# A sliding-window attention with a feed-forward layer: fewer idle matmuls, another order of loads, zeroing on GpSimd

## The chip, the cores and the metric

The kernel runs on one core of a Trainium2 chip. The metric is the device time of one execution in microseconds. Five runs of the kernel before were timed, and one execution was taken by the hardware profiler; all times on engines below come from that one.

## The reference

Attention over 8 batches of 8 heads, 576 positions and 64 numbers a head, with a causal mask: the first four heads see the last 32 positions, the other four see every fourth of the last 128. Then a feed-forward layer with a squared ReLU on the 4608 x 512 result.

```python
rel = pos[:, None] - pos[None, :]
mask_plain = (rel >= 0) & (rel < 32)
mask_dil = (rel >= 0) & (rel < 32 * 4) & (rel % 4 == 0)
scores = np.where(mask, scale * q @ k.T, -1e9)
attn = softmax(scores)
x = (attn @ v)            # heads side by side: 4608 x 512
h = np.maximum(x @ w_in, 0.0)      # w_in: 512 x 2048
out = (h * h) @ w_out              # w_out: 2048 x 512
```

## The kernel before

All order is written by hand. `PROGRAM` (lines 21 to 36) is a text of short codes, cut by `|`. What stands ahead of the first `|` is issued first; the part behind the (g+1)-th `|` is issued after feed-forward group g. An engine runs what it was given in that order, and waits where it needs another engine or a load. I write g0, g1 and so on for the groups.

**The groups.** The feed-forward layer works on tiles of tokens, 256 for the first four tiles and 512 after them. A group of the first product (`mm1`, L667) takes two columns of blocks of w_in at 256 tokens; its result is put through ReLU on ScalarE (L678) and squared on VectorE (L679). A group of the second product (`g2`, L699) is four 128x512 matmuls with one quarter of w_out: `part` p reads quarter p. After the fourth quarter ScalarE copies the sum (L705, to `osb`) and SyncE stores it. Groups g0 to g15 are the first product of tiles 0 and 1; g16 to g23 are the second product of tile 0, in the order quarter 0, 1, 0, 1, 2, 3, 2, 3 (two halves of the tile taken in turn). So g20 is the first to read w_out's third quarter and g21 the first to read its last. g24 to g31 are the second product of tile 1. Groups g2 and g3 are the first to read w_in's second quarter.

**The loads.** q, k, v and the weights come through GpSimd's DMA queue, which changes float32 to bfloat16 on the way. Codes such as `L1:q00123` mean: of batch 1, q and k of part 0, heads pairs 0 to 3 (two DMAs, L161). Part 0 is the first 256 positions of a batch, part 1 the other 320. `L0:i0` to `i3` are quarters of w_in (L753), `L0:o0` to `o3` quarters of w_out (L758), `v..d`, `p` and `r` are pieces of v (L184 or L191, L178, L197). q and k go to staging tiles `qb` and `kb`, of which there are three pairs (`rb`); batch 1 has the second, batches 0 and 2 share the first. v goes to `vd` and to the block-diagonal tile `vbd`, of which batches take two in turn.

**Batch 0, ahead of the groups (`first_step`).** For a pair of heads e and a part: `T` transposes q and k on TensorE (L495), `C` copies the result out of PSUM (`C..a` on ScalarE and VectorE, `C..v` on VectorE alone; L502 to L510), `B` writes the mask as a large negative number into a PSUM tile, with a matmul of the identity (L536), `S` adds the scores onto it (L555), `E` takes the exponential on ScalarE (L560), `P` and `D` are the products with v and with ones (L586, L602), `L`, `X` and `M` make the reciprocal and the product (L609, L612 on ScalarE, L619 on VectorE) and write `xT`, which group g0 reads. `B` takes one of four PSUM buffers named `pf` and needs nothing but the mask; the buffer comes free when an earlier `E` has read it.

**Idle matmuls.** `w21` and `W2`, `W3` and so on call `turn` (L457): that many matmuls of a zero tile, whose result nobody reads, 256 columns wide for `w` and 128 for `W`.

```python
elif code[0] in "wW":
    turn(int(code[1:]), 256 if code[0] == "w" else P)
```

**Batch 1 and later (`step`).** `1q2` is: q of head pair 2 of batch 1, part 0: transposes on TensorE (L235) into one of two PSUM buffers `pa`, then four copies (L248) on ScalarE for pairs 0 and 1, on VectorE for 2 and 3. `1k2` is the same for k (L252 or L259, VectorE). Capital letters are part 1. `1v3` spreads v on VectorE (L207), `1a2` is scores, exponential and mask (L310 or L304, L314, L315), `1o2` the product with v and its scaling (L413 to L428); `b` and `p` are `a` and `o` of part 1.

**Zeroing.** `z` zeroes the halves of the second `vbd` outside the diagonal blocks (`zero_halves`, L716 and L717). `y` zeroes rows 64 to 79 of part 0 in the staging tiles of batches 1 and 2 (L771, L772), since the transposes of a step read 80 rows. Both are VectorE work, issued after g15 and g17.

Of the kernel before, what the change touches and what calls it, by code (L numbers as in the profile page):

```python
# [19 lines left out]

PROGRAM = (
    "L0:q001 L0:q023 L0:q101 L0:q123 L0:v0d L0:v0p L0:i0 L0:v1dr L0:i1 L0:v1p L0:i2 L0:i3 L0:o0 L0:o1 L0:o2 "
    "L1:q00123 L0:o3 w21 T00 C00a T10 C10a B00 B10 W2 S00 E00 W3 S10 E10 W5 T20q W10 T20k C20v T30 C30v B20 "
    "B30 W3 S20 E20 W3 S30 E30 T01 C01v T11 C11v B01 B11 W2 S01 E01 T21 C21v S11 E11 T31 C31v B21 B31 P20 P30 "
    "D20 D30 L20 X20 M20 P00 P10 D00 D10 L00 X00 M00 S21 E21 S31 E31 W8 | | P21 P31 D21 D31 L21 X21 M21 L31 "
    "X31 M31 | | P01 P11 D01 D11 L01 X01 M01 L11 X11 M11 | | | | | | | | | | | | z | | y L1:v0dp L1:q10123 "
    "L1:v1dpr | | | | L2:q00123 L2:q10123 1q1 1q3 | 1q2 | 1k2 | 1k1 1v3 | 1a2 | 1v2 1k0 1q0 | 1o2 | 1a0 1a1 | "
    "1k3 1o0 1o1 | 1a3 1Q0 | 1K0 1o3 | 1Q1 1K1 | 1Q2 | 1b0 | | 1Q3 1K2 L2:vwpdr L3:q00123 L3:q10123 | L2:x | | "
    "2q0 | | 2k0 1V2 | 1b2 1p0 | 1b1 1V3 1K3 | | 1p2 1p1 | 2a0 1b3 | 2k1 2o0 2b0 1p3 | 2q1 2k2 L3:x | | 2q2 "
    "2p0 L3:vwpdr 2a1 | | | 2b1 | 2o1 2q3 2a2 | | 2p1 2v2 | 2k3 | 2b2 2o2 | 2v3 | 2a3 2p2 L4:q10123 | 2b3 3k1 "  # L30
    "| 2o3 3q1 | | 3a1 L4:q00123 2p3 | 3k0 3k2 | | 3o1 | | | 3q0 3v2 | | | | 3a0 | 3b1 3k3 | | | 3p1 L4:x 3q2 "
    "L4:vwpdr | | 3b0 | 3a2 3q3 3o0 4k0 | | | 3o2 3b2 | | 3p0 3v3 | 4q1 3a3 | 3p2 4q2 4q0 | L5:q10123 3b3 | "
    "3o3 | 4k1 | | L5:q00123 3p3 4k2 4k3 4a0 L5:vwpdr | | | 4b0 | | 4q3 | | 4o0 | | | 4a2 4v2 | 4b2 | 4a3 L5:x "
    "4a1 | 4o2 | | | 4p2 L6:q00123 4v3 | | 4b1 | | 4p0 | | 4p1 | 5q0 5k0 | 4b3 | | | | 4o1 | | 5k2 L6:q10123 "
    "4o3 | 5q2 5k1 | | 4p3 | 5q1 |"
)


# [25 lines left out]
def kernel(  # L64
# [9 lines left out]
    nc = tc.nc  # L74
    P = nc.NUM_PARTITIONS
    B, H, S, D = q.shape
# [66 lines left out]
    vbd = [const.tile([P, NE, NB, P], bf16, name=f"vbd{i}") for i in range(2)]  # L143
# [6 lines left out]
    def staged(b: int, nm: str):  # L150


        t = rb[STAGE[b]][nm]
        return t[:, :].rearrange("p (a h x) -> p a h x", h=H, a=2)

    def load_qk(b: int, part, es):
        hs = slice(2 * es[0], 2 * es[-1] + 2)
        for nm, src in (("q", q), ("k", k)):
            t = staged(b, nm)
            t0, n = RES * MS[part], MN[part]  # L160
            nc.gpsimd.dma_start(  # L161
                t[0:n, part, hs, :], src[b, hs, t0 : t0 + RES * n, :].rearrange("h (p r) d -> p h (r d)", r=RES)
            )

    def load_v(b: int, parts, which="pdr"):


        dst = vbd[b % 2]
        if b not in vds:
            vds[b] = vd_pool.tile([P, NE // 2, 2, RES * D], bf16, name="vd")  # L170
        p0, p1 = parts[0], parts[-1] + 1
        i0, i1 = 4 * p0, 4 if p1 == 1 else NB
        sides = [(hl, slice(64 * hl, 64 * hl + 64)) for hl in range(2)]
        for what in which:
            if what == "p":
                for e in range(NE // 2):
                    for hl, rows in sides:
                        nc.gpsimd.dma_start(  # L178
                            dst[rows, e, i0:i1, rows],
                            v[b, 2 * e + hl, 64 * i0 : 64 * i1, :].rearrange("(i p) d -> p i d", p=64),  # L180
                        )
            elif what == "d" and len(parts) == 1:
                for hl, rows in sides:
                    nc.gpsimd.dma_start(  # L184
                        vds[b][rows, :, p0, :],
                        v[b, H // 2 + hl : H : 2, 256 * p0 : 256 * p1, :].rearrange("e (p r) d -> p e (r d)", r=RES),
                    )
            elif what in "d01":
                for e in (0, 1) if what == "d" else (int(what),):
                    for hl, rows in sides:  # L190
                        nc.gpsimd.dma_start(  # L191
                            vds[b][rows, e, :, :],
                            v[b, H // 2 + 2 * e + hl, 0:512, :].rearrange("(m p r) d -> p m (r d)", p=64, r=RES),
                        )
            elif p1 == 2:
                for hl, rows in sides:
                    nc.gpsimd.dma_start(  # L197
                        dst[rows, NE // 2 : NE, 8, rows],
                        v[b, H // 2 + hl : H : 2, 512:S, :].rearrange("h p d -> p h d"),
                    )  # L200
# [231 lines left out]
    def step(b: int, code: str):  # L432

        what, e = code[0], int(code[1])
        part = int(what in "QKVbp")
        if what in "qk" and (b > XB or b == XB and e >= NE // 2):
            t = (qx if what == "q" else kx)[b % 2]
            by_act = what == "q" and e < NE // 2 and b < ADDED  # L440
            halves(
                e, what, t[:, 2 * e : 2 * e + 2, :, :], 0, M, nc.scalar.copy if by_act else nc.vector.tensor_copy
            )
        elif what in "qQkK":
            trans(b, e, what.lower(), part)
        elif what in "vV":
            spread_v(b, e, [part] if b in PARTED else [0, 1])
        elif what in "ab":
            scores(b, e, part)
        elif b in PARTED and e % 2:  # L450
            pv(b, e, part, ps_f, "pf")
        else:
            pv(b, e, part)
# [4 lines left out]
    def turn(n: int, cols: int):  # L458


        if "W" not in first:
            pool, nm = (ps_f, "pf") if ("P", 2, 0) in first else (ps_o, "po")
            first["W"] = pool.tile([P, 512], f32, name=nm)
        for _ in range(n):
            nc.tensor.matmul(
                first["W"][:, 0:cols], idle[:, 0:P], idle[:, 0:cols], start=True, stop=True, skip_group_check=True
            )
# [247 lines left out]
    def zero_halves(t):  # L715
        nc.vector.memset(t[0:64, :, :, 64:128], 0.0)  # L716
        nc.vector.memset(t[64:128, :, :, 0:64], 0.0)  # L717
# [45 lines left out]
    def cross_all(b):  # L763
        for part in range(2):
            for nm in "kq":
                cross(b, nm, part)

    def run(code):
        if code == "y":
            for nm in "qk":  # L770
                nc.vector.memset(staged(1, nm)[64:80, 0, :, :], 0.0)  # L771
                nc.vector.memset(staged(2, nm)[64:80, 0, 0 : H // 2, :], 0.0)  # L772
        elif code == "z":
            zero_halves(vbd[1])
        elif code[0] in "wW":
            turn(int(code[1:]), 256 if code[0] == "w" else P)
        elif code[0] in "TCBSEPDXM" or code[0] == "L" and code[2:3] != ":":
            first_step(code)
        elif code[0] != "L":
            step(int(code[0]), code[1:])  # L780
        else:
            b, what, part, which = int(code[1]), code[3], code[4:5], code[5:]
            if what == "q":
                load_qk(b, None if part == "w" else int(part), [int(e) for e in which])
            elif what == "x":
                cross_all(b)
            elif what == "v":
                load_v(b, [0, 1] if part == "w" else [int(part)], which)
            else:
                (load_w_in if what == "i" else load_w_out)(int(part))  # L790
# [22 lines left out]
    for code in program[0]:  # L813
        run(code)
    for g, group in enumerate(groups):
        for b in [x for x in CROSS if CROSS[x] == g]:
            cross_all(b)
        for b in [x for x in LOAD_V if LOAD_V[x] == g]:
            load_v(b, [0, 1])
        for b in [x for x in LOAD_QK if LOAD_QK[x] == g]:  # L820
            for part in range(2):
                load_qk(b, part, [0, 1, 2, 3])
        group()
        for code in program[g + 1] if g + 1 < len(program) else ():
            run(code)
        while steps and steps[0][0] <= g:
            step(*steps.pop(0)[1:])
# [30 lines left out]
```

## Time and profile before

| What | Value |
|---|---|
| five runs | 314.54, 318.08, 315.33, 317.29, 315.55 us; median 315.55 |
| the profiled execution | 314.54 us, its span 312.7 us |
| idle matmuls, 256 columns (L465) | 21, 4.3 us from 1.06 us on |
| idle matmuls, 128 columns (L465) | 28 into `po`, 2.7 us, and 8 into `pf`, 0.6 us |
| VectorE memsets z and y | 6, from 36.94 to 42.48 us |
| DMA issues on GpSimd, o3 | 24.55 us, lands 16.4 us later |
| DMA issues on GpSimd, q and k of batch 1, part 0 | 23.17 and 23.87 us, land 14.3 and 15.1 us later |

The page gives busy shares of each engine. PE is TensorE's matmuls and PEld its weight loads, which run beside them; DVE is VectorE, ACT ScalarE, POOL GpSimd, SP SyncE. A row of the timeline merges neighbouring instructions of a kind: its start, its length, engine, line, operation, output and input, count, and in brackets the idle time of the engine before it and what ended that. "x8" are eight instructions. The ends of matmuls are modelled, so rows of TensorE overlap a little. The time to landing is counted from the start of a DMA's issue.

### The profile page before, as it was taken

The page shows a single profiled execution, that of the slowest core. Times are in us where ns is not written, and L with a number is a line of the kernel's source. Part 1 is how long each engine was busy: PE and PEld are TensorE (multiplying, and loading weights), DVE is VectorE, ACT ScalarE, POOL GpSimd, SP SyncE. Part 2 cuts the span into 40 slices and gives each one's busy share as a digit, 9 for nine tenths or more (in the row PEclk, how much of TensorE's full clock was granted, in tenths as well). Part 3 has the DMA queues.
Part 4 walks back from the last instruction along what each step waited for, and adds up shares of the span by engine and source line. Part 5 has one row for each costly group of instructions (what it writes and reads, how often), then busy time and mean ns, then how long its engine had stood idle before and what let it go on. Part 6 is the DMA issues. An engine that isn't in the chain of part 4 may idle for free.

```text
span 312.7 us, 6856 instructions
## 1 busy us (share of the span) xinstructions
PE 302.9 (97%) x2605; PEld 190.0 (61%) x2605; DVE 200.3 (64%) x641; ACT 193.8 (62%) x416; POOL 87.0 (28%) x136
## 2 busy tenths in 40 slices
PE   8989989999999999999999999999999999999994
PEld 5779746968755555555499655555555555445543
DVE  6435587898987888985799469946995334104400
ACT  6377427859978956785478547864686456216511
POOL 8774276564265037401451041000000000000000
PEclk9999999999999999999999999999999999999999
DMA  8999999999979989995699975602200210121022
GB/s 115 155 166 214 204 145 179 184 135 200 152 141 193 180 106 214 141 187 66 89 140 140 141 120 100 109 4 66 69 0 2 68 68 2 34 67 36 0 67 67
DMA packets 79808, 34.91 MB, mean 112 GB/s; under 512 B 49824, under 2 KB 74784, under 8 KB 79776
## 3 DMA queue, kind: packets, MB, share of 16 engines
q0 software_dynamic: 47680, 18.36, 52.2%
q1 hardware_dynamic: 31952, 15.93, 26.1%
q8 instruction: 20, 0.33, 0.4%
q10 hardware_dynamic: 144, 0.20, 0.2%
q14 instruction: 12, 0.10, 0.1%
HBM read 36.90 MB, written 9.44 MB: 148 GB/s over the span
## 4 chain that ended last, share of the span: by engine, by line
PE 78%; DMA 10%; ACT 5%; POOL 3%; issue 2%; DVE 1%; ACTq 0%; POOLq 0%
PE pf L699 36%; PE pf L667 33%; DMA w_out_sb<-in_moe_w_out_dram 5%; PE po L413 3%; PE pd L415 2%; DMA w_in<-in_moe_w_in_dram 2%; DMA vd<-in_v_dram 2%; PE pa L304 2%; PE pa L310 1%; ACT qT L248 1%; POOL qb L161 1%; ACT h2T L678 1%; POOL kb L161 1%; PE pa L235 1%; ACT rec L417 1%
## 5 line engine op out<-in xcount | busy, mean ns | idle before, releaser
L699 PE MATMUL pf<-w_out_sb,h2T 128*128 128x512 bf16 (+1 forms) x592 | 134.8, 373 | 1.5 <-DMA w_out_sb<-in_moe_w_out_dram 1.0
L667 PE MATMUL pf<-xT,w_in 128*128 128x256 bf16 (+1 forms) x768 | 133.9, 326 | 1.8 <-DVE xT L619 1.2
L667 PEld LDWEIGHTS <-w_in 128*128 128x128 bf16 x768 | 82.4, 113 | 37.5 <-issue 2.8
L678 ACT ACTIVATE h2T<-pf 128x512 bf16<-128x512 f32 x144 | 83.7, 597 | 24.7 <-PE pf L667 23.7
L699 PEld LDWEIGHTS <-h2T 128*128 128x128 bf16 x592 | 54.2, 98 | 54.8 <-issue 1.9
L679 DVE TENSOR_TENSOR h2T<-h2T 128x512 bf16<-128x512 bf16 x144 | 57.9, 423 | 40.5 <-ACT h2T L678 39.0
L705 ACT COPY osb<-pf 128x512 f32<-128x512 f32 (+1 forms) x37 | 21.2, 573 | 47.3 <-PE pf L699 47.2
L428 DVE TENSOR_TENSOR xT<-po,rec 128x288 bf16<-128x288 f32 (+2 forms) x52 | 23.7, 456 | 31.5 <-ACT rec L418 30.9
L178 POOL DMA_DIRECT2D vbd<-in_v_dram x40 | 28.2, 725 | 52.3 <-PE pd L415 44.3
L417 ACT ACTIVATE rec<-pd 128x288 f32<-128x288 f32 (+2 forms) x52 | 21.5, 413 | 23.9 <-PE pd L415 22.9
L314 ACT ACTIVATE pt<-pa 128x352 bf16<-128x352 f32 (+6 forms) x56 | 27.6, 499 | 7.8 <-PE pa L310 4.1
L418 ACT ACTIVATE rec<-rec 128x288 f32<-128x288 f32 (+2 forms) x56 | 24.8, 443 | 1.8
L413 PEld LDWEIGHTS <-vbd 128*128 128x128 bf16 x286 | 17.0, 97 | 9.9 <-issue 0.7
L248 DVE COPY qT<-xx 64x288 bf16<-64x288 bf16 x80 | 19.9, 249 | 1.1
L161 POOL DMA_DIRECT2D qb<-in_q_dram x18 | 12.9, 719 | 23.0 <-DMA xx<-qb 17.6
L252 DVE COPY kbd<-xx 64x288 bf16<-64x288 bf16 x40 | 18.8, 470 | 0.6
L413 PE MATMUL po<-pt,vbd 128*128 128x96 bf16 (+3 forms) x263 | 18.0, 198 | 0.3 <-DVE vbd L207 0.2
L191 POOL DMA_DIRECT2D vd<-in_v_dram x24 | 14.5, 626 | 10.2 <-DMA qb<-in_q_dram 5.5
L415 PE MATMUL pd<-pt,mk 128*128 128x96 bf16 (+5 forms) x158 | 16.3, 204 | 0.0
L161 POOL DMA_DIRECT2D kb<-in_k_dram x18 | 12.8, 709 | 1.8 <-DMA w_out_sb<-in_moe_w_out_dram 1.2
L197 POOL DMA_DIRECT2D vbd<-in_v_dram x16 | 9.6, 604 | 11.0 <-PE pd L415 7.5
L304 PE MATMUL pa<-qT,kbd 128*128 128x96 bf16 (+2 forms) x146 | 12.2, 201 | 0.5 <-ACT qT L248 0.5
(81 smaller groups left out, 229.7 us busy)
## 6 DMA issues: line engine op xcount, KB each, us to landing
out_dram<-osb SPq DMA_DIRECT2D x18, 128.0 KB, 3.4
qb<-in_q_dram POOLq DMA_DIRECT2D x7, 320.0 KB, 7.5
kb<-in_k_dram POOLq DMA_DIRECT2D x7, 320.0 KB, 8.4
vd<-in_v_dram POOLq DMA_DIRECT2D x32, 64.0 KB, 6.0
w_in<-in_moe_w_in_dram POOLq DMA_DIRECT2D x4, 512.0 KB, 6.9
w_out_sb<-in_moe_w_out_dram POOLq DMA_DIRECT2D x4, 512.0 KB, 12.8
qb<-in_q_dram POOLq DMA_DIRECT2D x7, 256.0 KB, 5.6
kb<-in_k_dram POOLq DMA_DIRECT2D x7, 256.0 KB, 8.3
```

The costliest lines, as they stand in the source:

```text
L161: nc.gpsimd.dma_start(t[0:n, part, hs, :], src[b, hs, t0 : t0 + RES * n, :].rearrange("h (p r) d -> p h (r d)", r=RES))
L178: nc.gpsimd.dma_start(dst[rows, e, i0:i1, rows], v[b, 2 * e + hl, 64 * i0 : 64 * i1, :].rearrange("(i p) d -> p i d", p=64),)
L248: copy(qT[rows, e, :, m0 : m0 + n].rearrange("p (c j) m -> p j c m", j=2)[:, jj, :, :], src)
L314: nc.scalar.activation(pt[:, off : off + n], ps[:, 0:n], ACT.Exp, scale=SCALE)
L413: nc.tensor.matmul(oo, vb[:, e, i, :], rh, start=(x == 0), stop=(x == len(mms) - 1), skip_group_check=True)
L417: nc.scalar.activation(rec[:, 0:n], d[:, 0:n], ACT.Ln)
L418: nc.scalar.activation(rec[:, 0:n], rec[:, 0:n], ACT.Exp, scale=-1.0)
L428: nc.vector.tensor_tensor(out=tok, in0=o if o is o3 else o[:, 0:n], in1=rec if o is o3 else rec[:, 0:n], op=ALU.mult)
L667: nc.tensor.matmul(acc[u][:, nt * x + y0 : nt * x + y1], w_in_sb[piece][:, kt, c0 : c0 + 509 : 4], xT[:, kt, t0 : t0 + y1 - y0], start=(kt ...
L678: nc.scalar.activation(hv, acc[u][:, :].rearrange("p (x n) -> p x n", x=per), ACT.Relu)
L679: nc.vector.tensor_tensor(out=hv, in0=hv, in1=hv, op=ALU.mult)
L699: nc.tensor.matmul(cur[m][:, c0:c1], h2[:, f, P * m : P * m + P], w_out_sb[:, f, c0:c1], start=(f == 0), stop=(f == NF - 1),)
```

## The change

The text of codes is changed in its first stretch and around g15 to g23, and the zeroing moves to GpSimd.

- `L0:o3` stands ahead of `L1:q00123` (two DMAs) instead of behind it.
- `z`, `y` and then `L1:v0dp`, `L1:q10123` and `L1:v1dpr` are issued right after `L1:q00123`, ahead of batch 0's work, instead of after g15 and g17. On GpSimd's own queue the order of the loads stays the same but for o3; the six memsets are new there, between `L1:q00123` and `L1:v0dp`.
- `B20`, `B30`, `B01`, `B11` and `B21` come earlier among batch 0's steps, `B31` comes later, behind `M00`. The 128-column idle matmuls go from 36 to 16: W2, W3, W5, W10, W3, W3, W2, W8 become W5, W2, W3, W2, W4. `w21` stays.
- `1q1 1q3` are issued after g22 instead of g21, `1q2` after g23 instead of g22, in one place with `1k2`. From `1k1 1v3` on (after g24) all is as before.

```diff
-"... L0:o0 L0:o1 L0:o2 L1:q00123 L0:o3 w21 T00 C00a T10 C10a B00 B10 W2 S00 E00 W3 S10 E10 W5 T20q W10
- T20k C20v T30 C30v B20 B30 W3 S20 E20 W3 S30 E30 T01 C01v T11 C11v B01 B11 W2 S01 E01 T21 C21v S11 E11
- T31 C31v B21 B31 P20 P30 D20 D30 L20 X20 M20 P00 P10 D00 D10 L00 X00 M00 S21 E21 S31 E31 W8 | ...
- z | | y L1:v0dp L1:q10123 L1:v1dpr | | | | L2:q00123 L2:q10123 1q1 1q3 | 1q2 | 1k2 | 1k1 1v3 | ..."
+"... L0:o0 L0:o1 L0:o2 L0:o3 L1:q00123 z y L1:v0dp L1:q10123 L1:v1dpr w21 T00 C00a T10 C10a B00 B10 S00 E00
+ B20 S10 E10 B30 T20q B01 W5 T20k C20v T30 C30v B11 W2 S20 E20 W3 S30 E30 T01 C01v T11 C11v W2 S01 E01 T21
+ C21v B21 S11 E11 T31 C31v P20 P30 D20 D30 L20 X20 M20 P00 P10 D00 D10 L00 X00 M00 B31 S21 E21 S31 E31 W4
+ | ... | L2:q00123 L2:q10123 | 1q1 1q3 | 1q2 1k2 | 1k1 1v3 | ..."
@@ run(code)
         if code == "y":
             for nm in "qk":
-                nc.vector.memset(staged(1, nm)[64:80, 0, :, :], 0.0)
-                nc.vector.memset(staged(2, nm)[64:80, 0, 0 : H // 2, :], 0.0)
+                nc.gpsimd.memset(staged(1, nm)[64:80, 0, :, :], 0.0)
+                nc.gpsimd.memset(staged(2, nm)[64:80, 0, 0 : H // 2, :], 0.0)
         elif code == "z":
-            zero_halves(vbd[1])
+            nc.gpsimd.memset(vbd[1][0:64, :, :, 64:128], 0.0)
+            nc.gpsimd.memset(vbd[1][64:128, :, :, 0:64], 0.0)
```

## The prediction, on record before the result was known

> **What bounds the kernel now.** I read the page's busy shares first, then the table of stretches, then what TensorE waits for, and last the timeline around the two places that the change touches.
>
> ```profile
> PE 302.9 (97%) x2605; PEld 190.0 (61%) x2605; DVE 200.3 (64%) x641; ACT 193.8 (62%) x416; POOL 87.0 (28%) x136
> ```
> ```profile
> 10.00:15.00 5.00, 4.62 (x136) 3.56 (x135) 2.80 (x9) 1.91 (x4) 3.92 (x7) 1.00 1.28 145
> 17.50:20.00 2.50, 1.58 (x14) 1.42 (x14) 0.79 (x2) 1.85 (x4) 1.81 (x4) 1.00 1.33 187
> 30.00:35.00 5.00, 5.00 (x48) 5.00 (x47) 2.54 (x6) 3.34 (x7) 1.23 (x2) 1.00 1.10 208
> 40.00:45.00 5.00, 3.57 (x30) 1.85 (x30) 4.02 (x13) 1.71 (x6) 3.82 (x7) 1.00 1.34 134
> 100.00:160.00 60.00, 59.97 (x459) 34.04 (x458) 49.35 (x165) 41.02 (x88) 21.67 (x34) 1.00 1.01 140
> ```
> The columns are the stretch, its length, the busy time of PE, PEld, DVE, ACT and POOL, the granted clock, the DMA share and GB/s. TensorE is the bound almost everywhere: of 312.7 us it leaves 9.8 open, nearly all before 100 us and at the very end. So a microsecond taken from TensorE's path before 100 us reaches the end only if nothing else there is just as tight. The clock is 1.00 in every stretch, also where TensorE stood for 0.92 us of 2.50.
>
> TensorE's waits after 17 us (line, releaser, us, times, longest):
> ```profile
> PE pf L667 <- DVE xT L619: 1.2, 3, 0.8
> PE pf L699 <- DMA w_out_sb<-in_moe_w_out_dram: 1.0, 1, 1.0
> PE pa L235 <- ACT qT L248: 0.5, 1, 0.5
> ```
> The timeline in the head, and around the second and third of those waits (start, us, engine, line, what; in brackets the idle time before it and what ended it):
> ```profile
> 8.44 0.73 PE L465 MATMUL po<-idle 128*128 128x128 bf16 x10
> 9.10 0.31 PE L495 MATMUL pa<-mk,kb 64*64 64x64 bf16 x8
> ...
> 14.81 0.44 PE L586 MATMUL po<-pt,vd 64*64 64x64 bf16 x16
> ...
> 21.89 1.94 PE L667 MATMUL pf<-xT,w_in 128*128 128x256 bf16 x16
> ...
> 36.94 1.02 DVE L716 MEMSET vbd<- 64x1152 uint32 x1 [0.18 <-issue]
> 39.42 0.91 DVE L771 MEMSET qb<- 16x1024 uint32 x1 [0.16 <-issue]
> 40.94 1.02 PE L699 MATMUL pf<-w_out_sb,h2T 128*128 128x512 bf16 x4 [0.96 <-DMA w_out_sb<-in_moe_w_out_dram]
> 42.00 0.59 ACT L705 COPY osb<-pf 128x512 f32<-128x512 f32 x1 [5.70 <-PE pf L699]
> 42.49 1.07 ACT L248 COPY qT<-pa 64x128 bf16<-64x128 bf16 x4
> 42.50 0.93 DVE L248 COPY qT<-pa 64x128 bf16<-64x128 bf16 x4
> 43.61 0.30 PE L235 MATMUL pa<-mk,qb 80*128 80x80 bf16 x4 [0.49 <-ACT qT L248]
> 43.95 0.92 DVE L248 COPY qT<-pa 64x128 bf16<-64x128 bf16 x4 [0.53 <-PE pa L235]
> 49.70 0.50 PEld L304 LDWEIGHTS <-kbd 128*128 128x128 bf16 x8 [0.18 <-DVE kbd L252]
> ```
> And two pieces of the chain that ended last (start, us, what):
> ```profile
> 14.80 7.04 DMA w_in<-in_moe_w_in_dram
> ...
> 24.55 16.36 DMA w_out_sb<-in_moe_w_out_dram
> ```
> TensorE stands 0.96 us at 39.98 for the last quarter of w_out (group g21). And w_in's second quarter (i1), issued at 14.80, lands at 21.84, 0.05 us before g2, the first group that reads it, starts at 21.89.
>
> **The change part by part.** The sum is made against the profiled execution: 314.54 us, of which the span is 312.7; the median of the five runs shown is 1.01 us above it.
>
> *Idle matmuls and masks.* Ahead of P20 the idle 128-column matmuls fall from 28 to 12 (2+3+5+10+3+3+2 against 5+2+3+2), and from W8 to W4 behind E31. Ten of them move what follows from 8.44 to 9.10, so one is 66 ns: 16 x 66 = 1.06 us. Every B step is still run, but B31 (half of the 0.54 us from 14.27 to 14.81) moves behind M00, 0.27 us. Against this S01 has nothing left to hide its wait for the VectorE copies C01 (B01 and B11 stood there), some 0.5 us, and the first W2 only becomes part of the wait for the copies at 6.98. The transfers allow the advance: q and k of the first heads' second part landed at 8.5 and 10.0 (T01 ran at 10.84), those of T21 at 10.9 and 11.7 (12.53), v for P20 at 13.4 (14.81). So P20 goes from 14.81 to some 13.4 to 14.2, and with it the two ScalarE and VectorE chains that end at 18.80. But g2 needs i1, which the change does not touch: all loads up to o2 stay as they were on GpSimd's queue. TensorE then waits 0.6 to 1.3 us at 21.84 where it waited for nothing. I cost this part at 0.05 us gained. The cover is i1's landing; were it gone, the gain would be 1.3, and without any advance it is 0. Behind g2 all is tied to g2 (P01, D01, the 0.30 us wait at 26.88), so nothing comes back there.
>
> A rule speaks against this part. The rows give clock 1.00 in all stretches. The Trainium skill, "TensorE: Matmul & The Clock Gate", part 1, says that a window of about 3.4 us without activity halves TensorE's clock, and a busy one of that length restores it. My longest new gap is 1.3 us, so the row and the gap give 0; were one window nevertheless judged idle, an estimate from that page is half of 3.4 us, 1.7 us lost, and then only if it fell behind g2. I take 0 and keep 1.7 for the range.
>
> *w_out's last quarter (o3) ahead of batch 1's first q and k.* The queue lands in order: o2 at 36.4 (22.7 + 13.7), q at 37.5 (23.17 + 14.3), k at 39.0 (23.87 + 15.1), o3 at 40.9. Each of the 512 KB quarters o1 and o2 took 2.5 to 3.1 us after the one before it, o3 behind q and k 1.9. So o3 now lands at 38.3 to 39.5, ahead of 39.98, and the 0.96 us go. q and k land at 39.5 to 41.0 instead. What is late next: 1q1 and 1q3, now behind g22 (39.98 + 2 x 0.86 = 41.70), need q; 1k2 at about 43.4 needs k. Both have 1.5 us and more.
>
> What follows is the step that decides. 1q1 at 41.70 is only 0.1 us earlier than before (41.80). Its ScalarE copies started at 42.49 because the osb copy at 42.00 stood before them; that copy now belongs to g21's end at 40.85 and is over. So they run from about 42.05 to 43.12, and 1q2, which needs that PSUM buffer, comes at 43.16 instead of 43.61. From there VectorE is the bound: the copies of 1q2, 1k2, 1k1, 1v3, the mask of 1a2, 1v2 and 1k0 filled it from 43.95 to 49.65 with hardly a gap, and 1a0 waited for the last of them at 49.70. Begun at 43.5, the same 5.70 us end at 49.2. Of the 1.45 us of TensorE waits (0.96 + 0.49) only 0.45 to 0.5 thus reach 50 us; the rest turns into short waits for VectorE and ScalarE between 43 and 49. After 50 us the chain runs through compute alone, so the 0.5 is carried. Batch 2's transposed q and k are landed by 71 and first read at 76.4, those of batch 3 by 88.5 against some 92.6.
>
> *Zeroing (z, y).* VectorE loses 2 x 1.02 + 2 x 0.91 + 2 x 0.48 = 4.82 us between 36.94 and 42.48. It had nothing else there; only its first copy (42.50) came some 0.2 us late, contained in the above. GpSimd gets six memsets behind q and k of batch 1 (last issue over at 25.16) and ahead of L1:v0d. Its row has no such memset (only 128x1 ones, 0.10 us). From below: the VectorE rows, 4.8 us, or less. From above: the Trainium skill, "GPSIMD Engine Reference", section "Elementwise — side-by-side cycle accounting", puts its best tight loop at 1.8 cycles an element, and the engine at 1.2 GHz; for 2 x (2304 + 2048 + 1024) = 10752 bf16 elements a partition that is an estimate of 16.1 us, and at the 2.6 cycles that it gives for two inputs 23.3. The nearest row is VectorE's, so I take 5 to 10. Queued behind them are two loads v0d, four v0p, q and k of part 1, then batch 2's. They were issued at 26.02, 28.61, 31.05, 34.18, 36.68, 37.72, 39.27 and 41.19, each held back for an older transfer, and GpSimd stood idle for 10.4 of the 14.1 us from 25.2 to 39.3 (0.86 + 1.97 + 1.85 + 2.51 + 1.89 + 0.43 + 0.93). With 9 us of memsets the first goes at 34.4 and the queue has caught up by 37; they land behind k at 41 anyway, as before. Cost 0, hidden by the backlog o0 to k. The memsets need not wait for q's and k's landing: the v0p loads were issued from 31.05 on, before the memset at 36.94 that stands before them in the program and touches other rows and columns of the same tile, so disjoint regions make no wait.
>
> Sum: -0.05 - 0.45 + 0 = -0.5 us. Span 312.2, that execution 314.0, median 315.05.
>
> **The rivals.** *All of both waits comes through:* if the copies are less tight than I read them, 0.96 + 0.49 and 0.05 are gained, 314.05; if i1 also came early, up to 1.3 more, 312.8. For it: the chain names TensorE at most of 43.6 to 51; against it: the wait for VectorE at 49.70. *Nothing changes:* q or VectorE late by another half microsecond takes the 0.5 back, 315.5. *Slower:* the memsets hold GpSimd's queue. v0d's second load goes at 25.2 + T + 1.2 and lands 4.8 us later (as q at 39.27 did once the backlog was gone); 1v3 wants it at 46.6, and VectorE is in order, so 1k0 stands behind it. From T = 15.4 us each microsecond of T costs about one. At 16.1 it is 0.7, at 20 4.6 (319.6), at 23.3 7.9. It passes 1% above 315.55 from T = 19. Against it: 19 us is four times the VectorE rows.
>
> **How the numbers follow.** -0.5: 0.55. All comes through: 0.2, of which 0.05 beyond 1%, with the runs' scatter. Nothing: 0.1. Held queue or a clock window: 0.15, of which 0.12 over 1%. One percent is 3.2 us, what the five runs (314.54 to 318.08) can just tell from no change. So faster 0.05, same 0.83, slower 0.12. I predict 315.0; the range is 313.0 to 317.6: below, the full gain and some scatter, above, the lost 1.7 or T near 17.
>
> **What would show it.** Right: no wait of L699 for w_out at 40; a new wait of L667 for w_in of 0.6 to 1.3 us ending near 21.8; 1q2 near 43.2 and short waits for VectorE up to 49; GpSimd memsets of 5 to 10 us in all from 25.2, and v0p loads back at their times by 37. Wrong: g2 well before 21.8, memsets over 15 us, VectorE waiting for vd at 46, a clock below 1.00, or w_out still waited for.

## The result: 0.6% faster, nearly four times the gain that was forecast

The changed kernel took 313.75 us (median of 38 executions, 313.16 to 319.84), the kernel before 315.93 us (75 executions beside it, 313.99 to 319.04). The ratio is 0.9941, 95% interval 0.9926 to 0.9955, or 1.4 to 2.3 us gained. The forecast was 0.5 us, within 1%; 313.75 lies in the range of 313.0 to 317.6.

The profiled execution of the changed kernel took 313.40 us, its span is 311.4 us. The page's busy shares, as before:

```profile
PE 302.8 (97%) x2585; PEld 188.4 (61%) x2585; DVE 195.8 (63%) x635; ACT 194.1 (62%) x416; POOL 96.3 (31%) x142
```

What TensorE waited for between 17 and 100 us (line, releaser, us, times, longest):

```profile
PE pf L667 <- DVE xT L619: 1.0, 2, 0.7
...
PE pf L667 <- DMA w_in<-in_moe_w_in_dram: 0.2, 1, 0.2
...
PE pa L235 <- ACT qT L248: 0.2, 1, 0.2
```

The row for w_out is gone, and the 0.49 us in front of 1q2 are 0.16. The timeline at the places shown of before, with g16 to g21 in one row without a stop:

```profile
14.13 0.44 PE L586 MATMUL po<-pt,vd 64*64 64x64 bf16 x16
...
17.03 0.41 PE L667 MATMUL pf<-xT,w_in 128*128 128x256 bf16 x2 [0.24 <-DMA w_in<-in_moe_w_in_dram]
...
18.12 1.69 PE L667 MATMUL pf<-xT,w_in 128*128 128x256 bf16 x14 [0.68 <-DVE xT L619]
...
21.13 1.92 PE L667 MATMUL pf<-xT,w_in 128*128 128x256 bf16 x16
...
34.73 6.21 PE L699 MATMUL pf<-w_out_sb,h2T 128*128 128x512 bf16 x28
...
41.12 1.08 ACT L248 COPY qT<-pa 64x128 bf16<-64x128 bf16 x4 [0.42 <-PE pa L235]
...
42.25 0.30 PE L235 MATMUL pa<-mk,qb 80*128 80x80 bf16 x4 [0.16 <-ACT qT L248]
...
43.57 0.32 PE L235 MATMUL pa<-mk,kb 80*128 80x80 bf16 x4
...
48.56 0.49 PE L304 MATMUL pa<-qT,kbd 128*128 128x96 bf16 x8
```

and of before, g16 to g20 and 1a0:

```profile
35.50 4.48 PE L699 MATMUL pf<-w_out_sb,h2T 128*128 128x512 bf16 x20
...
49.86 0.48 PE L304 MATMUL pa<-qT,kbd 128*128 128x96 bf16 x8
```

P20 starts at 14.13 (before: 14.81), g2 at 21.13 (21.89), g16 at 34.73 (35.50), 1q2 at 42.25 (43.61), 1a0 at 48.56 (49.86). Of the 1.3 us at 1a0 about 0.8 were there at g2 and 0.5 came at w_out. From there the difference stays 1.3 us to the end of the spans (312.7 and 311.4). So between these two executions both halves of the change act, the head (all up to g15) and the place of o3, while the forecast gave the head 0.05 us. GpSimd's rows from the timeline:

```profile
24.22 2.08 POOL L774 MEMSET vbd<- 64x2304 bf16 x1
26.34 2.01 POOL L775 MEMSET vbd<- 64x2304 bf16 x1
28.30 1.80 POOL L771 MEMSET qb<- 16x2048 bf16 x1
30.05 0.94 POOL L772 MEMSET qb<- 16x1024 bf16 x1
30.94 1.80 POOL L771 MEMSET kb<- 16x2048 bf16 x1
32.69 0.94 POOL L772 MEMSET kb<- 16x1024 bf16 x1
33.58 1.22 POOL L184 DMA_DIRECT2D vd<-in_v_dram  x2
...
36.54 0.61 POOL L178 DMA_DIRECT2D vbd<-in_v_dram  x1 [0.49 <-DMA w_out_sb<-in_moe_w_out_dram]
```

The six memsets take 9.57 us, and the loads behind them are back at their old times by 36.54 (third v0p, before 36.68). The next ones, the fourth v0p and q and k of part 1, go at 39.00, 40.42 and 41.71, later than before (37.72, 39.27, 41.19). That is not the memsets: in the changed kernel with the zeroing on VectorE they go at 38.84, 40.31 and 41.64.

### The profile page after: what moved, and what is told of

It reads as the page before. It is cut to its first block, busy times and chain, and to the rows that moved or that the text cites. A ratio compares the mean times of both kernels' runs of the same rounds, so it can differ in the third digit from the quotient of the medians.

```text
span 311.4 us, 6816 instructions
## 1 busy us (share of the span) xinstructions
PE 302.8 (97%) x2585; PEld 188.4 (61%) x2585; DVE 195.8 (63%) x635; ACT 194.1 (62%) x416; POOL 96.3 (31%) x142
## 4 chain that ended last, share of the span: by engine, by line
PE 87%; ACT 6%; DVE 4%; issue 2%; ACTq 0%
PE pf L667 37%; PE pf L699 37%; PE po L413 3%; PE pd L415 2%; PE pa L304 2%; PE po L465 2%; PE pa L310 1%; ACT h2T L678 1%; ACT qT L248 1%; DVE kbd L252 1%; PE pa L495 1%; ACT rec L417 1%; PE pa L235 1%; ACT rec L418 1%; DVE xT L428 1%
## 5 line engine op out<-in xcount | busy, mean ns | idle before, releaser
L428 DVE TENSOR_TENSOR xT<-po,rec 128x288 bf16<-128x288 f32 (+2 forms) x52 | 23.7, 457 | 31.0 <-ACT rec L418 30.5
```

The costliest lines, as they stand in the source:

```text
L428: nc.vector.tensor_tensor(out=tok, in0=o if o is o3 else o[:, 0:n], in1=rec if o is o3 else rec[:, 0:n], op=ALU.mult)
```

## The experiments

Ten kernels ran beside the changed one, and two of the kernels twice, each with the kernel before on the same chip. "Full clock" are the executions whose mean granted clock was at least 0.9975; the last column counts the others, most of them at 0.993 to 0.995, a few at 0.988 to 0.992.

| Kernel | median us | ratio to before (95%) | median at full clock | below full clock |
|---|---|---|---|---|
| before, in the three sets | 316.4, 316.3, 316.5 | 1 | 315.7, 315.7, 315.8 | 53 of 151 |
| changed | 313.75 | 0.9941 (0.9926 to 0.9955) | 313.6 | 9 of 39 |
| changed, again | 313.54 | 0.9918 (0.9892 to 0.9944) | 313.5 | 2 of 15 |
| masks alone | 316.19 | 1.0010 (0.9991 to 1.0028) | 315.6 | 11 of 22 |
| o3 alone | 314.14 | 0.9946 (0.9927 to 0.9966) | 314.1 | 0 of 7 |
| zeroing alone | 316.89 | 1.0013 (0.9992 to 1.0033) | 315.9 | 13 of 22 |
| changed, without the masks | 314.42 | 0.9953 (0.9932 to 0.9973) | 314.4 | 2 of 22 |
| changed, g2 without i1 | 313.68 | 0.9917 (0.9895 to 0.9939) | 313.6 | 4 of 22 |
| the same, without the masks | 314.06 | 0.9935 (0.9908 to 0.9963) | 314.1 | 0 of 10 |
| changed, 1q1 behind g21 | 313.66 | 0.9929 (0.9908 to 0.9951) | 313.5 | 3 of 22 |
| changed, zeroing on VectorE | 313.44 | 0.9914 (0.9882 to 0.9946) | 313.4 | 0 of 6 |
| the same, again | 313.33 | 0.9906 (0.9875 to 0.9938) | 313.3 | 0 of 6 |
| before, o3 later | 318.51 | 1.0067 (1.0044 to 1.0091) | 317.0 | 16 of 20 |
| before, wait filled | 316.46 | 0.9992 (0.9970 to 1.0013) | 316.5 | 0 of 14 |

### The masks alone

```diff
- w21 T00 C00a T10 C10a B00 B10 W2 S00 E00 W3 S10 ... S31 E31 W8
+ w21 T00 C00a T10 C10a B00 B10 S00 E00 B20 S10 ... S31 E31 W4
```

> Only the steps of batch 0 are reordered and the idle matmuls go from 36 to 16; o3 stays behind q and k, zeroing stays on VectorE. My theory after the result: the masks bring g2 forward by 0.6 to 0.8 us (from 21.9 to about 21.2), but alone they gain nothing, since o3 still lands near 40.9: TensorE then stands about 1.7 us for w_out at g21 instead of 0.96, ratio 0.998 to 1.001. My prediction's step (g2 is held by i1's landing near 21.84): g2 at 21.8, wait for w_out 1.0, ratio 1.000. Rival, that the whole gain comes from the head: ratio near 0.994.

Nothing is gained (1.001), as the theory after the result said, but not quite for its reason. The two largest waits of TensorE in this profile from 15 to 100 us:

```profile
PE pf L699 <- DMA w_out_sb<-in_moe_w_out_dram: 1.9, 1, 1.9
PE pf L667 <- DMA w_in<-in_moe_w_in_dram: 1.6, 2, 1.0
```

and the timeline:

```profile
17.50 2.04 PE L667 MATMUL pf<-xT,w_in 128*128 128x256 bf16 x16 [0.97 <-DMA w_in<-in_moe_w_in_dram]
...
21.82 1.94 PE L667 MATMUL pf<-xT,w_in 128*128 128x256 bf16 x16 [0.64 <-DMA w_in<-in_moe_w_in_dram]
...
41.81 1.02 PE L699 MATMUL pf<-w_out_sb,h2T 128*128 128x512 bf16 x4 [1.90 <-DMA w_out_sb<-in_moe_w_out_dram]
```

In this execution the head's gain went, as the prediction said, into waits for w_in, 0.97 for the first quarter and 0.64 for the second; and whatever had passed would have ended in the wait for o3.

### o3 alone

```diff
- L1:q00123 L0:o3
+ L0:o3 L1:q00123
```

> Only o3 stands ahead of q and k of batch 1; 1q1 and 1q3 stay behind g21. My theory: no wait for w_out at g21 (0.96 gone), VectorE then carries about 0.5 us of it past 50 us, ratio about 0.9984 (-0.5 us). Rival, that all of the two waits comes through: -1.4 us, 0.9955. Rival, that q is late for 1q1 at 40.85: no gain, with a wait of L235 for qb.

0.9946, 1.7 us: about the rival's number, and most of the whole change. But not for the rival's reason. In its timeline g16 to g21 now run without a stop, and 1q2 still waits:

```profile
36.17 5.34 PE L699 MATMUL pf<-w_out_sb,h2T 128*128 128x512 bf16 x23
...
43.16 0.30 PE L235 MATMUL pa<-mk,qb 80*128 80x80 bf16 x4 [0.49 <-ACT qT L248]
...
49.97 0.49 PE L304 MATMUL pa<-qT,kbd 128*128 128x96 bf16 x8
```

From g16 to 1a0 it is 13.80 us here, 13.83 in the changed kernel (34.73 to 48.56) and 14.36 before (35.50 to 49.86): of the 0.96 some 0.55 get past the copies, as I said, and q was there in time for 1q1. What was larger than I said must be the wait itself.

### How large is the wait for o3?

In five profiles of kernels with o3 behind q and k, device time less the start of g21 is nearly the same: before 314.54 - 40.94 = 273.6, masks alone 315.84 - 41.81 = 274.0, zeroing alone 317.19 - 42.81 = 274.4, wait filled 316.68 - 42.80 = 273.9, o3 later 316.96 - 43.38 = 273.6. In all five g21 waits for o3; two of the rows, of zeroing alone and of wait filled:

```profile
42.81 1.02 PE L699 MATMUL pf<-w_out_sb,h2T 128*128 128x512 bf16 x4 [1.68 <-DMA w_out_sb<-in_moe_w_out_dram]
```

```profile
42.80 1.02 PE L699 MATMUL pf<-w_out_sb,h2T 128*128 128x512 bf16 x4 [1.59 <-DMA w_out_sb<-in_moe_w_out_dram]
```

The landing of o3 thus sets the time to within 0.8 us, and it ranges over 2.4 (1.9 without o3 later). Before's median at full clock, 315.7, then belongs to a g21 near 41.8: an estimate of 1.8 us of waiting in the typical execution, where the one with a profile had 0.96. This takes the end of g20 from that profile, 39.98, and it moves too: it is 39.9 to 41.1 in the five. A second estimate needs no such choice. In o3 alone the device time less the start of g16 is 314.65 - 36.17 = 278.5; the other profiles with an early o3 give 278.2 to 278.9, but for two in which a transfer came late behind 60 us. Its median of 314.1 then belongs to a g16 at 35.6, so g20 would end at 40.1 and the wait be 1.7 us.

The kernel with o3 put later tests this:

```diff
- L1:q00123 L0:o3 ... y L1:v0dp L1:q10123
+ L1:q00123 L1:v0dp L0:o3 ... y L1:q10123
```

> The kernel before, with o3 behind the six loads L1:v0dp as well. If o3's landing sets the time: a longer wait for w_out at g21, and device time minus o3's landing near 274 us as in the profiles of before (273.6), masks alone (274.0) and zeroing alone (274.4); so 1.5 to 4 us slower than before. If other work absorbs the wait: less than half of the added wait shows in the time.

```profile
43.38 1.02 PE L699 MATMUL pf<-w_out_sb,h2T 128*128 128x512 bf16 x4 [2.41 <-DMA w_out_sb<-in_moe_w_out_dram]
```

At 273.6 the profile keeps the rule. The time rose by 2.1 us at the ratio, but by 1.2 among executions at full clock, which were only four; 16 of 20 were below it.

### Do the masks help once o3 is early, and does i1 hold g2?

The changed kernel with batch 0's steps of before:

> The changed kernel with batch 0's steps and idle matmuls as before. My theory: o3 and zeroing together give about -0.5 to -0.8 us, ratio 0.9975 to 0.9985, g2 near 21.9; the missing part against 0.9941 is what the masks add once o3 is early (0.7 us or more). Rival, that masks add nothing (g2 held by i1): ratio 0.994 as the whole change.

314.42 against 313.75: the masks add about 0.7 us, in separate sets and with overlapping intervals. The gain left without them, 0.9953, is again above the 0.9975 to 0.9985 that I expected, as with o3 alone. Then the same pair with g2 and g3 of tile 0 reading w_in's first quarter, so that these kernels leave w_in's second quarter out there:

```diff
                 f = per * u + x
+                if tk0 == 0 and u in (2, 3):
+                    f -= 4
```

> The changed kernel, with g2 and g3 (second quarter of the hidden columns for the first 256 tokens) computed from w_in's first quarter, so that g2 no longer waits for i1. If i1's landing holds g2 in many runs of the changed kernel: no wait of L667 for w_in at g2, g2 directly behind D31, and 0.2 to 0.6 us less than the changed kernel's 313.75, ratio to before about 0.992 to 0.993. If TensorE's own order holds g2: the same as the changed kernel, 0.994.

> The same edit with batch 0's steps and idle matmuls as before. If i1 was what hid the masks' gain: this stays at the 0.995 of the run without masks, within 0.001, as D31 ended with i1's landing there, and the difference to the run with masks grows to 0.8 to 1.2 us. Rival, that the masks give little of themselves: the two with g2 freed are within 0.3 us.

Without i1 in its way the changed kernel is at 313.68, with it at 313.75 and 313.54: freeing g2 gains nothing that these medians show, so I take it that i1's landing does not hold g2 in the typical execution. In some it does: by 0.64 us in the profile of the masks alone and by 0.40 in the second profile of the changed kernel, and in the profile of this run g2 starts at 21.12 while i1 lands at about 21.6. How often that happens in executions without a profile stays open. The pair on one chip differs by 0.4 us (313.57 and 314.06, so 0.5, at full clock): less than the 0.8 to 1.2 expected. By both pairs the masks are worth about half a microsecond, an estimate, since the intervals overlap in both. Their cover, i1's landing, is partial and changes from execution to execution: i1 landed at 21.8 in the profile of before, at 21.0 in that of the changed kernel, and between 20.6 and 23.7 over all profiles.

### The place of 1q1 and 1q3

```diff
- L2:q00123 L2:q10123 | 1q1 1q3 | 1q2 1k2 |
+ L2:q00123 L2:q10123 1q1 1q3 | 1q2 | 1k2 |
```

> The changed kernel with 1q1 and 1q3 behind g21, 1q2 behind g22, 1k2 behind g23, as before. If VectorE's chain of copies is the bound from 42 to 50 us and q has landed: 0.3 to 0.8 us faster than the changed kernel, as the first copy comes one group earlier (about 40.3). If q and k land after 40: a wait of L235 for qb or kb, and no gain or a loss of up to 0.5 us.

313.66: no difference from the changed kernel. The profile shows the second case:

```profile
39.24 1.02 PE L699 MATMUL pf<-w_out_sb,h2T 128*128 128x512 bf16 x4 [0.32 <-DMA w_out_sb<-in_moe_w_out_dram]
...
40.68 0.45 PE L235 MATMUL pa<-mk,qb 80*128 80x80 bf16 x8 [0.42 <-DMA qb<-in_q_dram]
```

q of batch 1, now behind o3, lands at 40.55 (issued at 22.39, 18.16 us to landing); one group later it is there in time. Even early, o3 holds g21 by 0.32 us here, where g16 began earliest of all profiles, at 34.44.

### The zeroing

Alone on the kernel before:

> Only the zeroing moves to GpSimd, with the loads behind it as in the changed kernel; o3 stays behind q and k. My theory: memsets of about 9.5 us from 24.9, loads back at their times by about 37, the first copies at 42.5 some 0.2 us earlier, ratio 0.999 to 1.000. Rival, that GpSimd's queue is held and loads come late: ratio above 1.002, with TensorE or VectorE waiting for vd or vbd.

and taken back out of the changed kernel, twice:

```diff
-                nc.gpsimd.memset(staged(1, nm)[64:80, 0, :, :], 0.0)
+                nc.vector.memset(staged(1, nm)[64:80, 0, :, :], 0.0)
```

> The changed kernel with z and y on VectorE again, behind g15 and g17; loads in the same order. My prediction put the zeroing at nothing but 0.2 us of VectorE's start: the memsets now run from about 36.2 to 41.7, the first copy of q comes at 41.7 instead of 41.27, so 0.2 to 0.5 us slower than the changed kernel, ratio about 0.995. Rival, that GpSimd's memsets cost as much by holding the loads: the same or faster, 0.993 to 0.994.

> The changed kernel once more, beside the next one: 313.4 to 314.0, TensorE's wait for w_out 0.

> The changed kernel with z and y on VectorE, once more. If GpSimd's memsets are worth nothing or cost a little: the median is within 0.3 us of the changed kernel's or below it. If they are worth the 0.2 to 0.5 us that I first expected: it is that much above.

Alone it gives 1.0013, no difference, and in its profile neither TensorE nor VectorE waits for a load of v up to 60 us. Taken back, the medians are 313.44 and 313.33 against 313.75 and 313.54: not slower, perhaps 0.2 faster, inside the scatter. In the first of these profiles the copies do start late, behind the memsets (41.93 against 41.27):

```profile
41.44 0.48 DVE L772 MEMSET kb<- 16x512 uint32 x1
41.93 1.89 DVE L248 COPY qT<-pa 64x128 bf16<-64x128 bf16 x8
43.85 0.94 DVE L259 COPY kbd<-pa 64x128 bf16<-64x128 bf16 x4
```

VectorE's rows of the changed kernel for the same work:

```profile
42.59 0.92 DVE L248 COPY qT<-pa 64x128 bf16<-64x128 bf16 x4 [0.40 <-PE pa L235]
...
45.79 0.58 DVE L207 COPY vbd<-vd 64x256 bf16<-64x256 bf16 x2
...
46.60 0.63 DVE L207 COPY vbd<-vd 64x256 bf16<-64x256 bf16 x2
```

Yet 1a0 starts at 48.56, as in the changed kernel, though g16 came 0.21 us later (34.94): the two batches of copies ran without the 0.40 us gap that stood between them there, and the two copies of v behind them took 0.46 and 0.45 us instead of 0.58 and 0.63. Why the copies of v were shorter is not shown. The move to GpSimd is not what makes the change faster. The kernel with o3 early, the masks and VectorE's memsets beats the one before and is at least level with the changed one.

### The granted clock

In a third of before's executions (53 of 151) the mean clock was lower, mostly near 0.995. One stretch of 3.4 us at half clock, as the trace below has it, makes 0.9946 of a span of 312 us. To see whether the wait for o3 does it, 24 idle matmuls were put in it:

```diff
- ... (behind g20) |
+ ... (behind g20) W24 |
```

> The kernel before, with 24 idle matmuls of 128 columns (about 1.5 us) behind g20, where TensorE waits for o3. If idling there is what lowers the granted clock in about a third of the executions of before (0.995 against 1.000, 1.4 us longer): such executions become rare (under a tenth), the median falls by 0.3 to 0.6 us, and those at clock 1.0 stay at 315.7. If the clock falls elsewhere: still a third, median the same or up to 0.5 us worse.

None of 14 was below full clock, against 16 of 44 beside them; with o3 later it was 16 of 20, with o3 early 20 of 149 over all such kernels. So waiting there does lower the clock in part of the executions. But the median did not fall: those at full clock lie at 316.5 and not at 315.7. The idle matmuls have a cost of their own: they end at about 41.2, and g21 cannot start before.

```profile
39.71 1.50 PE L465 MATMUL pf<-idle 128*128 128x128 bf16 x24
```

By the rule above a g21 at 41.2 is 315.1 us, and the fastest of the 14 took 315.10, where the fastest of before beside them took 314.17. That takes the fastest executions away, but cannot raise a median that lies above 315.1. Nor do those below full clock look like the ones with the longest waits: their medians lie 1.7 to 1.9 us above those at full clock in the three sets, and 3.4 us at half clock can cost 1.7. Why none of the saving appears stays open. The one profile of the kernel before shows no such execution. The second run of the changed kernel does, at another place. Its page and its timeline:

```profile
PEclk9999999999997999999999999999999999999999
```

```profile
93.44 1.75 ACT L248 COPY qT<-xx 64x288 bf16<-64x288 bf16 x4 [1.57 <-DMA xx<-qb]
...
95.25 0.32 PE L304 MATMUL pa<-qT,kbd 128*128 128x96 bf16 x4 [2.12 <-ACT qT L248]
```

and the stretches around it (PE, PEld, DVE, ACT, POOL, clock, DMA share, GB/s):

```profile
92.00:94.00 2.00, 1.12 (x6) 0.34 (x3) 1.55 (x4) 0.55 (x2) 0.07 (x1) 1.00 0.70 184
94.00:96.00 2.00, 0.75 (x14) 0.75 (x15) 0.79 (x2) 1.95 (x5) 2.00 (x3) 1.00 0.32 13
96.00:98.00 2.00, 2.00 (x8) 0.84 (x7) 1.33 (x4) 0.92 (x3) 2.00 (x4) 0.66 1.18 151
98.00:100.00 2.00, 1.78 (x12) 1.09 (x12) 1.88 (x7) 1.86 (x4) 2.00 (x4) 0.50 1.39 181
100.00:102.00 2.00, 2.00 (x10) 1.03 (x9) 1.91 (x9) 1.66 (x5) 0.90 (x2) 0.99 1.31 241
```

Batch 3's transposed q came after 93, TensorE stood 2.12 us and was busy for only 1.87 of the 4 us from 92 to 96, and from about 96.6 the clock was at half for some 3.4 us. That execution took 316.73 us. Such a gap does not always lower the clock: o3 later's profile has one of 2.41 us and the masks alone one of 1.90 us, and the clock stays 1.00 in the stretches behind them, up to 52 and 48 us.

## Why the prediction was right in its mechanism and short in size

**The wait for w_out, the mis-sized term.** "the 0.96 us go" was right of the profiled execution. It was wrong as a term of a sum that was then moved to the median by a constant ("median 1.01 us above it"): by the estimates above that microsecond is itself mostly the wait, not a constant. The profiled execution was the fastest of the five, and by the rule of the five profiles this is because o3 landed early in it. The typical wait is 1.7 to 1.8 us. What exceeds 0.96 shifts g21 and everything behind it and passes whole: 315.7 - 314.5 = 1.2, with the 0.45 of the next step 1.6. o3 alone gave 1.7 by its ratio, 1.6 at full clock. That 313.75 still lies in the range is luck in part: its lower end, 313.0, was drawn for the rival in which both waits come through, not for a longer wait.

**VectorE's chain, right.** I said that of 0.96 + 0.49 only 0.45 to 0.5 get past 50 us. Between the two profiles 1a0 gained 1.3, of which 0.8 was there at g2; 0.5 remain. Freed of the head, the stretch from g16 to 1a0 shortened by 0.53 and, with o3 alone, 0.56.

**The head, half right.** P20 came at 14.13, inside the 13.4 to 14.2 forecast. "g2 needs i1" and its price in a new wait were seen in the masks alone (0.64, and 0.97 for i0 that I had not named). But I took i1's landing of one execution, 21.84, as fixed. It moves over 3 us; in the changed kernel's profile it was early, and g2 came at 21.13, "well before 21.8", one of my own signs of being wrong. Freed of i1 the kernel is no faster. So 0.05 should have been about 0.5.

**The zeroing, right.** It cost nothing. The memsets took 9.57 us, in the bracket of 5 to 10; the loads were back by 37; no memset waited for q's landing. The upper end of 16.1 us did not occur: 9.57 us for 10752 elements are 0.89 ns each, 1.07 cycles of 1.2 GHz. The 16.1 came from the 1.8 cycles that the Trainium skill, "GPSIMD Engine Reference", section "Elementwise — side-by-side cycle accounting", gives as the best case of "a tight unroll-4 loop". The same paragraph has 1.03 cycles an element for short loop bodies ("k ≤ 2"), which makes an estimate of 9.2 us; which of the two holds for a memset it does not say, and the measurement decides for the second.

**What is late next, right but closer than I said.** In the changed kernel's profile o3 lands at 38.7, where I gave 38.3 to 39.5, q at 40.1 and k at 41.4, where I gave 39.5 to 41.0 for both. 1q1 starts at 40.78 and 1k2 at 42.39, so 0.6 and 1.0 us are left, not the "1.5 us and more". Batch 3's transposed q, which I had read as landed by 88.5, came after 93 in the second run.

**The clock rule.** I looked for it in the head, where no stretch of the changed kernel's profile is below 1.00. By the counts above it acts where the kernel before waits for o3, and in one trace where transposed q is late. There the longest gap was 2.12 us, shorter than the 3.4 us window that the Trainium skill names in "TensorE: Matmul & The Clock Gate", part 1; the length of the drop, some 3.4 us, fits that window.

**Of the rivals,** "all of both waits comes through" named a number near the measured one, 314.05, by another way; the held queue did not occur.

## What to carry to other kernels

A wait for a transfer in one profile is one draw. Where the runs of a kernel spread over more than the effect looked for, ask first whether the spread is that wait, by setting device time against the landing in several profiles; what is gained is then the typical wait, not the one seen. A gain in front of a gate is worth nothing until the gate is opened: the masks gave 0 alone and about half a microsecond behind an early o3, so parts of a change are to be tried in pairs too. And work put on an idle engine because another is busy is worth checking by putting it back.

## What the runs showed of the hardware that was not expected

- The same load in the same place of the queue was issued between 14.0 and 16.0 us and landed between 20.6 and 23.7 us (i1, fourteen profiles of twelve kernels, on several chips).
- TensorE's clock fell to half 1.4 us after a gap of 2.12 us had ended, and stayed there for some 3.4 us; after a gap of 2.41 us in another profile it did not fall.
- GpSimd cleared 64x2304 bfloat16 in 2.0 to 2.1 us, where VectorE took 1.02 us for the same bytes, which it wrote as 64x1152 words of 32 bits; GpSimd's rows stay in bfloat16, at nearly the same time an element.
